# The first load of a scale-and-add kernel: descriptors of 4 KB instead of 8 KB

One Trainium2 chip, one core. The metric is the device time of one execution in microseconds, lower is better. All runs quoted are of one state (fast; the granted clock was 1.0 in each).

## The reference

```python
B, S, D = 1024, 16, 512          # x, y: bf16 [1024, 16, 512]; gamma: bf16 [512]
def reference(x, y, gamma):
    return x + gamma * y
```

x and y are 16.8 MB each, and the result is as large: 50.33 MB have to pass between HBM and the core's memory, with very little arithmetic.

## The kernel before

The 16384 rows of 1 KB are cut into three blocks so that each of the 128 partitions has 8, 60 and 60 rows, contiguous in HBM. One transfer moves one block. All loads go through one queue (SyncE's), all stores through another (ScalarE's, together with gamma).

```python
BLOCKS = [8, 60, 60]
# ... (cut)
SP = [                       # loads in this order: tensor, first row, end row, (place in x's buffer)
    ('y', 0, 8),
    ('y', 8, 68),
    ('x', 8, 68, 0),
    ('y', 68, 128),
    ('x', 68, 128, 15),
    ('x', 0, 8, 0),
]
ACT = [('g',), ('s', 8, 68), ('s', 68, 128), ('s', 0, 8)]     # gamma, then the stores
EARLY = (2, 0)               # the first two loads stand at the head of the program
RELEASE = ('x', 68, 128, 15) # stores may start when this load has landed
DVE = [('m', 0), ('m', 1), ('m', 2), ('a', 2), ('a', 1), ('m', 3), ('a', 3), ('a', 0)]
# ... (cut)
            elif kind == "x":
                to = x_sb[:, w[3] : w[3] + w[2] - w[1], :]
                i = eng.dma_start(out=to, in_=rows_of(xf, w[1], w[2])).then_inc(s_load[w], 16)
            elif kind == "y":
                r = slice(w[1], w[2])
                i = eng.dma_start(out=y_sb[:, r, :], in_=rows_of(yf, w[1], w[2])).then_inc(s_load[w], 16)
            else:
                r = slice(w[1], w[2])
                i = eng.dma_start(out=rows_of(of, w[1], w[2]), in_=y_sb[:, r, :]).then_inc(s_out, 16)
```

VectorE multiplies pieces of y by gamma in place ("m") and adds x to them ("a"); gamma is spread over the partitions by one matmul.

## Time and profile before

| | before |
|---|---|
| time, median of 3 runs | 119.86 us (119.83 to 119.91) |
| span of the profiled run | 118.5 us |
| share of the 16 DMA engines' time in packets | 65.8% + 32.7% |
| VectorE busy | 59% |
| first packet starts / first load landed | 1.04 / 4.82 us |
| last packet ends / last store landed | 118.11 / 118.50 us |

The first two rows tell how fast the program is; the third tells why. The other times are in us from the issue of the first load; those with two decimals are from the trace's records of packets and of semaphore increments. A load or store has landed when the last of its 16 increments is recorded. The lines themselves are in the prediction.

### The profile page before, as it was taken

What the parts mean: (1) busy time and instruction counts of PE and PEld (TensorE: products, weight loads), DVE (VectorE), ACT (ScalarE), POOL (GpSimd) and SP (SyncE); (2) the same over time, 40 slices, a digit from 0 to 9 for tenths busy, and PEclk for the clock granted to TensorE, in tenths of its full rate; (3) what the DMA queues carried; (4) which work ended last, traced back from release to release, by engine and by line L of the source; (5) the groups of instructions that cost most, each with busy time, mean ns of one, the idle gap of its engine ahead of it and who ended that gap; (6) DMA issues with size and microseconds to landing.
All of it is one profiled execution on the core that took longest, in us unless ns stands there. A gap on an engine that the chain in (4) does not pass through costs nothing. (4 is left out here: it accounts for less than half of the span.)

```text
span 118.5 us, 81 instructions
## 1 busy us (share of the span) xinstructions
PE 0.6 (0%) x1; PEld 0.1 (0%) x1; DVE 70.1 (59%) x10; POOL 0.2 (0%) x4
## 2 busy tenths in 40 slices
PE   0001000000000000000000000000000000000000
PEld 0000000000000000000000000000000000000000
DVE  0005400299999399999499999469999950000000
POOL 0000000000000000000000000000000000000000
DMA  5999779779779779978977977897797797797787
GB/s 180 506 602 394 332 332 663 332 332 663 332 332 663 332 332 601 394 332 352 643 332 332 663 332 332 384 633 332 332 663 332 332 663 332 332 663 332 332 365 321
DMA packets 1298, 50.33 MB, mean 425 GB/s; under 512 B 145, under 2 KB 146, under 8 KB 146
## 3 DMA queue, kind: packets, MB, share of 16 engines
q1 hardware_dynamic: 864, 33.55, 65.8%
q10 hardware_dynamic: 434, 16.78, 32.7%
HBM read 33.56 MB, written 16.78 MB: 425 GB/s over the span
## 5 line engine op out<-in xcount | busy, mean ns | idle before, releaser
L170 DVE TENSOR_TENSOR y_sb<-y_sb,gamma_sb 128x4096 bf16<-128x4096 bf16 (+3 forms) x4 | 34.7, 8689 | 11.9 <-DVEq L33 11.9
L179 DVE TENSOR_TENSOR y_sb<-x_sb,y_sb 128x23040 bf16<-128x23040 bf16 (+3 forms) x4 | 34.6, 8688 | 4.5 <-DVEq L33 4.5
L146 DVE CAST gamma_sb<-gamma_ps 128x512 bf16<-128x512 f32 x1 | 0.7, 690 | 7.9 <-DVEq L33 7.9
L141 DVE MEMSET ones_row<- 1x128 bf16 x1 | 0.2, 165 | 2.0 <-PEq L49 2.0
L144 PE MATMUL gamma_ps<-gamma_row,ones_row 1*128 1x512 bf16 x1 | 0.6, 581 | 9.3 <-PEq L33 9.3
L144 PEld LDWEIGHTS gamma_ps<-gamma_row,ones_row 1*128 1x128 bf16 x1 | 0.1, 97 | 9.3 <-issue 9.3
L208 POOL MEMSET const-bfloat16-1.0<- 128x1 bf16 x1 | 0.1, 102 | 0.0
L208 POOL MEMSET const-uint8-127<- 128x1 uint8 x1 | 0.1, 102 | 0.0
L208 POOL MEMSET const-float32-0.0<- 128x1 f32 x1 | 0.1, 99 | 0.2 <-issue 0.2
L208 POOL MEMSET const-float32-1.0<- 128x1 f32 x1 | 0.1, 99 | 0.0
## 6 DMA issues: line engine op xcount, KB each, us to landing
y_sb<-in_y_dram SPq DMA_DIRECT2D x2, 7680.0 KB, 39.8
x_sb<-in_x_dram SPq DMA_DIRECT2D x2, 7680.0 KB, 31.5
out_dram<-y_sb ACTq DMA_DIRECT2D x2, 7680.0 KB, 21.0
y_sb<-in_y_dram SPq DMA_DIRECT2D x1, 1024.0 KB, 4.8
x_sb<-in_x_dram SPq DMA_DIRECT2D x1, 1024.0 KB, 22.3
out_dram<-y_sb ACTq DMA_DIRECT2D x1, 1024.0 KB, 22.1
gamma_row<-in_gamma_dram ACTq DMA_DIRECT2D x1, 1.0 KB
```

The lines of the kernel that those rows point to most:

```text
L141: nc.vector.memset(ones_row, 1.0).then_inc(s_ones, 1)
L144: nc.tensor.matmul(gamma_ps, ones_row, gamma_row, start=True, stop=True).then_inc(s_ps, 1)
L146: nc.vector.tensor_copy(out=gamma_sb, in_=gamma_ps).then_inc(s_dve, 1)
L170: nc.vector.tensor_tensor(out=yt, in0=yt, in1=g, op=MULT).then_inc(s_dve, 1)
L179: nc.vector.tensor_tensor(out=yt, in0=xt, in1=yt, op=ADD).then_inc(s_add, 1)
L208: nc = _bacc.Bacc("TRN2", target_bir_lowering=False, num_devices=1)
```

## The change

The intent is to let the first load run in smaller pieces: 8 contiguous rows of a partition, 8 KB, become two descriptors of 4 KB. (A descriptor is one contiguous piece of a transfer; the trace records each as one packet.) Bytes, order, waits and all other transfers stay as they are.

```diff
+FIRST_BYTES = 4096
@@
             elif kind == "y":
                 r = slice(w[1], w[2])
-                i = eng.dma_start(out=y_sb[:, r, :], in_=rows_of(yf, w[1], w[2])).then_inc(s_load[w], 16)
+                cap = FIRST_BYTES if w == y_loads[0] else None
+                i = eng.dma_start(out=y_sb[:, r, :], in_=rows_of(yf, w[1], w[2]), max_dma_last_dim=cap).then_inc(s_load[w], 16)
```

## The prediction

> **What bounds the kernel now.** I read the page's header and busy lines first, then the slices, then the table of DMA queues, then the waits, then the timeline of VectorE, and at last the DMA view in short windows.
>
> ```profile
> DVE  0005400299999399999499999469999950000000
> DMA  5999779779779779978977977897797797797787
> DMA packets 1298, 50.33 MB, mean 425 GB/s; under 512 B 145, under 2 KB 146, under 8 KB 146
> q1 hardware_dynamic: 864, 33.55, 65.8%
> q10 hardware_dynamic: 434, 16.78, 32.7%
> y_sb<-in_y_dram SPq DMA_DIRECT2D x1, 1024.0 KB, 4.8
> ```
>
> VectorE has empty slices at both ends and gaps between. The two DMA queues together take 65.8% + 32.7% = 98.5% of the time of all 16 DMA engines. The 7s in the slice line are an artefact: a packet is booked where it starts, and most packets here last almost a slice (shown below). 1298 packets are what the kernel's shapes give if one contiguous row of a partition is one packet: nine transfers x 128 = 1152, one for gamma, and 145 of 4 bytes which tell of the end (9 x 16 + 1). So the first load is 128 packets of 8192 bytes, 8 on each engine. In the trace's packet records I chained each packet to the one that ended within 12 ns of its start: this gives 16 chains, 3.146 MB each, with no gap above 20 ns from an engine's first packet (1.035 to 1.832 us) to its last (ends 117.84 to 118.11 us). The kernel is 16 DMA engines that work without a pause, and whichever ends last sets the time.
>
> The waits and the timeline tell how much room VectorE has:
>
> ```profile
> DVE y_sb L170 <- DVEq L33: 11.9, 3, 9.8
> 11.02 2.29 DVE L170 TENSOR_TENSOR y_sb<-y_sb,gamma_sb 128x4096 bf16<-128x4096 bf16 x1 [0.26 <-DVEq L33]
> 23.10 16.23 DVE L170 TENSOR_TENSOR y_sb<-y_sb,gamma_sb 128x7680 bf16<-128x7680 bf16 x2 [9.79 <-DVEq L33]
> 41.36 16.23 DVE L179 TENSOR_TENSOR y_sb<-x_sb,y_sb 128x23040 bf16<-128x23040 bf16 x2 [2.04 <-DVEq L33]
> 59.40 16.16 DVE L170 TENSOR_TENSOR y_sb<-y_sb,gamma_sb 128x30720 bf16<-128x30720 bf16 x1 [1.81 <-DVEq L33]
> ```
>
> The first load lands at 4.8 us, its multiply starts only at 11.02 us because gamma comes late (its semaphore fills at 9.2 us), and after it VectorE is idle 9.8 us until the second y load lands (22.96 us by the trace). Every later stretch starts with an idle gap that a landing ends. So neither the first load nor its multiply is urgent; what counts of the first load is how long it holds the DMA engines.
>
> **What the Trainium skill says.** (1) "DMA: Bandwidth & Descriptors", Where 436 GB/s comes from: 435 GB/s is the ceiling of 16 ports. The trace agrees: 425 GB/s over the whole span. (2) Same page, Why small descriptors are slow (HBM only): a fixed overhead of about 3 cycles for each packet,[...] which matters for packets of a few hundred bytes.[...] (3) Same page, The descriptor swizzle: engines 0 to 7 serve partitions 0 to 63, engines 8 to 15 the others, four partitions in a row each, and hardware generation splits the same way. The trace fits: the 16 chains start in two groups of eight, 1.035 to 1.450 us and 1.667 to 1.832 us, as if descriptors were made in the order of partitions. (4) Same page, Queues, rings and completion order: engines alternate between queues at packet boundaries only. That fits gamma's wait: issued at 1.9 us on the other queue, its 1 KB packet starts at 6.56 us, after a packet of 61440 bytes, and its semaphore packet starts at 8.87 us, one such packet later.
>
> **The change part by part.** Instruction for instruction both programs are the same on every engine; only the first load's pattern turns from 128x4096 into 128x2x2048 elements.
>
> *Removed and added packets.* 128 packets of 8192 bytes go, 256 of 4096 bytes come: 16 on each engine instead of 8. The cost of one comes from two windows of the before trace, the first with packets of 8192 bytes alone (2.5 to 4 us), the second with 61440 bytes alone (60 to 76 us):
>
> ```profile
> DMA packets 77, 0.63 MB, mean 421 GB/s; under 512 B 0, under 2 KB 0, under 8 KB 0
> q1 hardware_dynamic: 77, 0.63, 99.6%
> ...
> DMA packets 112, 6.88 MB, mean 430 GB/s; under 512 B 0, under 2 KB 0, under 8 KB 0
> q1 hardware_dynamic: 112, 6.88, 99.2%
> ```
>
> 16 engines x 1.5 us x 99.6% / 77 = 310 ns for 8192 bytes; 16 x 16 us x 99.2% / 112 = 2267 ns for 61440 bytes. The packet records say 309 and 2267, with each start 3 ns before the previous end, so 306 and 2264 from start to start. The difference, 1958 ns for 53248 bytes, is 27.2 bytes per ns; 8192 bytes at that rate are 301 ns, so about 5 ns are fixed. A packet of 4096 bytes should then take 150.6 + 5 = 155.6 ns start to start, and 16 of them 2490 ns against 8 x 306 = 2448 ns: **+0.04 us** on every engine. As no engine ever pauses, this is fully on the path: +0.04 us of 119.86, or 0.03%.
>
> *Moved: the landing of the first load.* 4.8 us becomes about 4.86 us. VectorE wants it at 11 us, so this costs nothing.
>
> *Moved: gamma.* Its place in the alternation may change, since packet boundaries on the first load come every 156 ns instead of 306. If gamma's packet gets in before the first packet of 61440 bytes, gamma lands up to 4.7 us earlier (about 4.5 us instead of 9.2), and the first multiply starts near 6.3 us. It would then only idle longer until 22.96 us: no gain.
>
> *Moved: the ramp.* This is the one part whose size I cannot work out. At present the first packets take 361 to 1108 ns instead of 309, yet all end between 2.05 and 2.28 us; taking off 309 ns, data flow begins on all engines between 1.74 and 1.97 us, wherever they started. If the cause is a common delay before the first data, smaller descriptors change nothing. I take this as the most likely, and the sum is **+0.04 us, 119.90 us**. I put the point a little higher, at 119.95, because the first rival below is larger than the second.
>
> **The rivals.**
> *The generator is slow for each descriptor.* The eight later engines start 0.632 us after the eight earlier ones (1.667 against 1.035), the last 0.797 us after the first. If this is the pace at which descriptors are made, about 64 of them between engine 0 and engine 8 (9.9 ns each), then twice as many make engine 8 start at 1.035 + 1.264 = 2.30 us, and engine 15 at 1.035 + 1.594 = 2.63 us. With the 52 to 146 ns which these later engines need before data flows, their flow begins at about 2.35 to 2.75 us instead of 1.74 to 1.97: +0.6 to +0.8 us, never made up because each engine has its fixed share and the last one sets the end. Time: 120.5 to 120.7. For it: the two groups. Against it: the flow begins at one common moment although the early group started 0.6 us before, and from the second packet on no engine is short of descriptors. About 35%.
> *The first data flows earlier.* If a first packet must be read whole before the write starts, half the size saves up to half of 301 ns: -0.15 + 0.04, 119.75 us. Against it: the shortest first packet took 361 ns, only 52 over a later one, so there is little left to save. About 20%.
> *VectorE or the release of the stores becomes the bound.* The stores' release follows the landing of the last large x load (77.4 us), which moves with the stream itself. VectorE has 1.8 us or more of idle time ahead of each later stretch. I see no way in which this could cost anything: under 3%, some tenths of a us.
>
> **Range and chances.** Neutral gives 119.85 to 120.0 (45%), the slow generator 120.5 to 120.7 (35%), the early flow about 119.7 to 119.8 (20%); runs of the kernel before lie within 0.08 us. I predict 119.95 us, 8 in 10 within 119.65 and 120.65. Two per cent is 2.4 us, or the whole time for which the first load holds the engines; no rival comes near. Faster 1%, same 98%, slower 1%.
>
> **What would show it right or wrong.** The header should count 1426 packets, 402 of them under 8 KB, and queue q1 992. A window within the first load should give about 156 to 159 ns a packet and a rate near 420 GB/s; a much lower rate there means a fixed cost above my 5 ns. The landing of the first load tells the ramp: about 4.86 us if neutral, 4.7 if the flow starts earlier, 5.4 to 5.6 if generation is slow, and then with eight engines that start after 2.2 us. The second y load's landing (22.96 us) and the last store should move by the same amount. The first multiply may start at 6 us or at 11 us without any effect on the end. I am wrong if the chains of packets get pauses after the first load, if packets of 61440 bytes change from 2267 ns, or if the end moves by more than the first load's landing does.

## The result, and the profile after

The changed kernel took 120.07 us (median of 6 runs, 120.02 to 120.15) against 119.88 us (6 runs, 119.76 to 120.05): ratio 1.0014, 95% interval 1.0001 to 1.0027. A ratio here is the mean time of one kernel's fast runs over that of the other's of the same rounds, so it is not quite the ratio of the quoted medians. Twice more on other occasions (below) the ratio was 1.0009 and 1.0008. So the change costs 0.1 to 0.2 us: the same within 2%, and if anything slower.

The header, the load queue and the landing of the first load on the page of the kernel after (the queue's columns are packets, MB, share of the 16 engines' time; the last line's are KB and us from issue to landing):

```profile
DMA packets 1426, 50.33 MB, mean 424 GB/s; under 512 B 145, under 2 KB 146, under 8 KB 402
q1 hardware_dynamic: 992, 33.55, 65.9%
y_sb<-in_y_dram SPq DMA_DIRECT2D x1, 1024.0 KB, 5.0
```

The counts are the ones foreseen, 128 packets more, and the load's landing is at 5.0 us instead of 4.8. Its packets, in a window of the DMA view of the kernel after from 2.3 to 3.6 us, where all of them are of this load:

```profile
DMA packets 130, 0.53 MB, mean 410 GB/s; under 512 B 0, under 2 KB 0, under 8 KB 130
q1 hardware_dynamic: 130, 0.53, 99.7%
```

16 engines x 1.3 us x 99.7% / 130 = 160 ns for 4096 bytes, where nearly all records say 159: the working's 155.6 from start to start, and the 3 ns by which packets overlap in the records. VectorE's timeline of the kernel after, to be set beside the one of before (start, duration, instruction, and in brackets the idle time ahead of it):

```profile
11.20 2.29 DVE L173 TENSOR_TENSOR y_sb<-y_sb,gamma_sb 128x4096 bf16<-128x4096 bf16 x1 [0.26 <-DVEq L35]
23.27 16.23 DVE L173 TENSOR_TENSOR y_sb<-y_sb,gamma_sb 128x7680 bf16<-128x7680 bf16 x2 [9.77 <-DVEq L35]
41.53 16.23 DVE L182 TENSOR_TENSOR y_sb<-x_sb,y_sb 128x23040 bf16<-128x23040 bf16 x2 [2.04 <-DVEq L35]
59.56 16.16 DVE L173 TENSOR_TENSOR y_sb<-y_sb,gamma_sb 128x30720 bf16<-128x30720 bf16 x1 [1.80 <-DVEq L35]
```

Every start is 0.16 to 0.18 us later than before, and the idle times ahead are the same to 0.02 us. The shift is there when the first load lands (4.99 against 4.82 us), and at the second load's landing (23.13 against 22.96) it is the same (0.17 us). Nothing is lost or won back by VectorE.

What was not foreseen is in a view that I had not opened before predicting: the first issue by itself, before and then after (durations in ns: min/median/max of this one instruction).

```profile
L130 SPq DMA_DIRECT2D y_sb<-in_y_dram x1: 372/372/372, 0.0 to 0.0; - x1
```

```profile
L133 SPq DMA_DIRECT2D y_sb<-in_y_dram x1: 425/425/425, 0.0 to 0.0; - x1
```

The instruction that issues the first load now takes 425 ns instead of 372, and the first packet starts at 1.095 instead of 1.035 us.

### The profile page after: what moved, and what is told of

The parts are those of the page before. It is cut to its first block, busy times and chain, and to the rows that moved or that the text cites. A ratio compares the mean times of both kernels' runs of the same rounds, so it can differ in the third digit from the quotient of the medians.

```text
span 118.7 us, 81 instructions
## 1 busy us (share of the span) xinstructions
PE 0.6 (0%) x1; PEld 0.1 (0%) x1; DVE 70.1 (59%) x10; POOL 0.2 (0%) x4
```

## The experiments

**Theory after the result.** Three parts: a longer issue at the very head of the program (+0.05 us), the packets (+0.04 us), and a more uneven start of the 16 engines. **Rivals:** chance; packets of 4 KB that cost more than 5 ns each and explain it alone; a descriptor generator that is slow for each descriptor.

For all but the repeats, the size was made a table, used for loads (and in one run for the stores):

```diff
-FIRST_BYTES = 4096
+CAPS = {...}                 # (tensor, first row, end row): bytes
-    ... max_dma_last_dim=cap)
+    ... max_dma_last_dim=CAPS.get(w[:3]))
```

Results, each against the kernel before on the same chip (medians; n runs):

| run | CAPS or edit | us | ratio (95%) |
|---|---|---|---|
| before_again | none | 119.94 (5) | 1.0002 (0.9988 to 1.0015) |
| after_again | the change | 120.05 (5) | 1.0009 (0.9997 to 1.0022) |
| after_third | the change | 120.02 (6) | 1.0008 (0.9991 to 1.0025) |
| first_2k | y 0..8: 2048 | 120.21 (6) | 1.0023 (1.0005 to 1.0041) |
| first_1k | y 0..8: 1024 | 120.50 (5) | 1.0047 (1.0034 to 1.0059) |
| last_4k | x 0..8: 4096 | 119.95 (6) | 1.0000 (0.9982 to 1.0018) |
| last_1k | x 0..8: 1024 | 120.41 (5) | 1.0040 (1.0027 to 1.0052) |
| big_first_8k | order of first two loads | 120.19 (5) | 1.0018 (1.0004 to 1.0031) |
| big_first_4k | the same, y 0..8: 4096 | 120.32 (4) | 1.0028 (1.0015 to 1.0042) |
| big_first_1k | the same, y 0..8: 1024 | 120.59 (4) | 1.0056 (1.0042 to 1.0070) |
| loads_4k | all loads but the first: 4096 | 124.28 (6) | 1.0362 (1.0349 to 1.0375) |
| stores_4k | both large stores: 4096 | 121.96 (4) | 1.0171 (1.0151 to 1.0191) |

Before was 119.91, 119.90 and 119.89 us (medians).

**The repeats.** No edit; the kernels before and after once and twice more.

> The kernel before, unchanged, to learn how well it repeats and how its ramp varies. Every theory: ratio to before 1.000 within 0.0015. In the profile I expect data to flow on the 16 engines from 1.74 to 1.97 us again (spread near 0.24 us) and the first load's landing at 4.80 to 4.85 us. If the spread comes out as anything between 0.2 and 0.5 us, the uneven start after the change is chance and not its doing.

> The changed kernel, unchanged. Main theory: the loss of about 0.19 us has three parts, packets +0.04, a longer issue of the first load (425 instead of 372 ns, +0.05), and a more uneven start of the engines (data flow from 1.64 to 2.08 us instead of 1.74 to 1.97, +0.05 to +0.1 on the latest). It should repeat: +0.1 to +0.25 us, first packet near 1.09 us, four engines that start after 2.0 us. Rival (noise): the time is within 0.05 us of before and the profile's ramp looks like that of before.

> The changed kernel a third time, for its scatter: time +0.1 to +0.2 us; first issue 415 to 425 ns, first packet 1.07 to 1.10 us, landing of the first load 4.95 to 5.05 us. If the latest engine's data flow begins below 2.06 us here, the more uneven start seen in the first two profiles is chance, and the loss is issue and packets alone.

The loss repeats in sign and is 0.13 to 0.19 us by the medians, though two of the three intervals reach 1. The profiles separate it better. There are six starts with a first load of 8 KB packets (before, before_again, and four runs below whose change comes later) and three of the changed kernel; in us:

| | first load in 8 KB (6 profiles) | in 4 KB (3 profiles) | difference of means |
|---|---|---|---|
| first issue takes | 0.361 to 0.382 | 0.412 to 0.425 | +0.044 |
| first packet starts | 1.002 to 1.035 | 1.061 to 1.095 | +0.055 |
| data flow begins on the latest engine | 1.97 to 2.15 | 2.08 to 2.18 | +0.09 |
| last packet of the first load ends | 4.428 to 4.600 | 4.566 to 4.619 | +0.09 |
| first load landed, latest engine | 4.76 to 4.96 | 4.956 to 4.992 | +0.13 |

The times are from the trace's records; data flow on an engine begins at the end of its first packet less the time that one of its later packets takes. The times of the issue and of the first packet do not overlap between the two groups. The start of the latest engine does; most of its +0.09 is the 0.055 of the later first packet, and the rest is within what two executions of one kernel differ by. So the uneven start that I read out of the first pair of profiles is not established: the spread alone (0.24 us before) was 0.77 us in before_again, where flow began on different engines between 1.29 and 2.06 us; I had expected 0.24 again. By the mark that I had set for after_third (below 2.06 us would have shown it to be chance) it was not refuted either: 2.18 us. But in after_third some engines moved a first packet by 1.35 us and paused afterwards; counted back from the last packet's end (4.576 us, 16 packets of 155.6 ns), the latest start is 2.09 us. Counted back in the same way in all nine, the latest start moves by +0.05 us in the means, as the first packet does.

**More descriptors in the same place.** 2 KB and 1 KB.

> First load in descriptors of 2 KB, 32 packets an engine. Main theory: issue near 420 ns as with 4 KB and 1 KB, so it belongs to the added dimension and not to the number of descriptors, +0.06 us; packets 32 x (75.3 + 4.9) = 2.57 us, +0.12 us; landing of the first load at 5.0 to 5.1 us; time +0.15 to +0.3 us. Rival (issue or start grows with the number of descriptors): first packet after 1.15 us, first load landing after 5.2 us.

> First load in descriptors of 1 KB, 64 packets an engine instead of 8. Main theory: 64 x (37.7 + 4.9) ns = 2.72 us against 2.45, +0.28 us; issue +0.05; uneven start +0.1 to +0.3 if it grows with the number of descriptors: together +0.4 to +0.65 us, about 120.3 to 120.5. Rival (a packet costs more than 5 ns, all of the loss of the change is packets: 0.19 us / 8 = 24 ns each): 56 x 24 = +1.3 us. Rival (generation at 9.9 ns for each descriptor, the slow generator of the prediction): 1024 x 9.9 = 10 us for the first load, +7 us or more.

The first packets start at 1.097 and 1.090 us, with issues of 425 and 417 ns: the same as with 4 KB. So the longer first issue goes with the added dimension of the pattern, not with the number of descriptors. What does grow with their number is the issue of the second load, right behind it: 424 ns in before, 459 or 460 in the three runs with 4 KB, 497 with 2 KB, 568 with 1 KB; its packets are not wanted before 4 us. With 2 KB the first load lands at 5.06 us, as the main theory expected. Nor is generation the bound: 1024 descriptors are handled with the first load landing at 5.3 us, by the issue table of first_1k:

```profile
y_sb<-in_y_dram SPq DMA_DIRECT2D x1, 1024.0 KB, 5.3
```

At the 9.9 ns each that I had taken from the staggered starts, they would have needed 10 us. The slow generator is ruled out. The times, +0.3 and +0.6 us, are at the upper end of what the main theory expected. In first_1k the records show one reason: packets of 1 KB take 46 ns until 4.0 us, then 49 to 52 in the mean, with VectorE idle and no packet of another queue under way.

**The same bytes where the issue is off the path.** The last load, x 0..8, is issued at 57.6 us and its packets run from 76.5 us.

> The change's own descriptor size on the other small load: the last one, whose issue is long past when its turn comes, in 4 KB; the first stays at 8 KB. Main theory (of the change's loss some 0.06 us is the longer issue of a first instruction with one more dimension, 0.04 us packets, the rest start scatter): first issue 372 ns and first packet at 1.00 to 1.04 us as before, +0.04 us in the end, too little to tell from before by time. Rival (the loss belongs to packets of 4 KB wherever they are): +0.15 us or more. It also adds another start with 8 KB packets.

> First load at 8 KB as before; instead the last load (the same 8 rows of x), whose issue and descriptors are ready long before its turn, in descriptors of 1 KB. Main theory: packets alone, +0.28 us, nothing for issue or start; the difference from first_1k is then what the place at the start of the program costs. Rival (a packet costs 24 ns): +1.3 us. Rival (only the start costs anything): 0. The landing of the last load should move by the same amount, that of all earlier loads not at all.

The added dimension lengthens this issue as well (383 ns in last_1k and last_4k, 328 in before), but 20 us ahead of need. It does so for both large stores too (407 and 379 ns in stores_4k, 369 and 339 in before), but not for a load issued right behind another: 423 to 434 ns in second place, with the dimension (big_first_4k, big_first_1k, loads_4k) and without. last_4k: 119.95 us, +0.06 by the medians, ratio 1.0000; of its 256 packets the mean was 159.8 ns. By time it cannot be told from before, while the change in the first place reads +0.13 to +0.19; but its interval, 0.2 us either way, doesn't exclude that. last_1k cost 0.5 us instead of the 0.28 expected. Its packets say why: up to 78 us they followed each other every 42.3 ns as worked out, then slowed. The DMA view in two windows of last_1k, 76.9 to 77.8 us and 78.6 to 79.4 us:

```profile
DMA packets 335, 0.33 MB, mean 372 GB/s; under 512 B 8, under 2 KB 335, under 8 KB 335
q1 hardware_dynamic: 335, 0.33, 105.0%
...
DMA packets 275, 0.28 MB, mean 352 GB/s; under 512 B 0, under 2 KB 275, under 8 KB 275
q1 hardware_dynamic: 275, 0.28, 110.5%
```

16 x 0.9 us x 105.0% / 335 = 45 ns recorded in the first (46 in the records, with 8 short semaphore packets in the mean), 16 x 0.8 x 110.5% / 275 = 51 ns in the second.

**The small load second in the queue.** The edit:

```diff
 SP = [
-    ('y', 0, 8),
     ('y', 8, 68),
+    ('y', 0, 8),
-DVE = [('m', 0), ('m', 1), ('m', 2), ...
+DVE = [('m', 1), ('m', 2), ('m', 0), ...
```

> The order of the first two loads turned round: the 60 rows of y first (one packet of 61440 bytes per partition), the 8 rows second, still 8 KB each; their multiplies follow in the same order. The small load is then neither in the ramp nor is its issue on the path. Main theory (the small load at the head of the queue only costs what its packets, issue and start cost): bytes and packet counts are those of before, so within 0.1 us of before. Rival (a small first load is what makes the engines start sooner): +0.2 us or more. It is the base for the next two runs.

> As big_first_8k, with the 8 rows of y, now second in the queue, in descriptors of 4 KB. Main theory: 8 more packets an engine at 4.9 ns, +0.04 us against big_first_8k, as issue and start are no longer on the path; the landing of this load and the next moves by 0.03 to 0.06 us. Rival (packets of 4 KB cost the whole 0.17 us that the change cost wherever they stand): +0.17 us in the landings against big_first_8k.

> As big_first_8k, with these 8 rows in descriptors of 1 KB, at a time when no other queue has work. In last_1k the packets took 42.3 ns from start to start until 78.1 us and up to 57 later, once the store's queue was filled. Main theory (the extra there comes of a second queue or of VectorE's reads beside it): here all take about 42.3 ns, the load holds an engine 64 x 42.3 = 2.71 us, +0.26 us against big_first_8k. Rival (packets of 1 KB vary anyway): +0.45 us as in last_1k.

big_first_8k was 0.3 us slower than before. Its profile shows one engine on which data flow began only at 2.61 us, the next at 2.10; but this is the slowest of its five runs (120.46; the others 120.04 to 120.21), so a single profile doesn't settle a cause. I had expected no difference; a small load at the head seems to be worth about 0.2 us here (ratio 1.0018), and why is not settled. big_first_4k: the runs scatter too much (119.99 to 120.41 us) to show 0.04 us, and its profile fell on the fastest. The packets are clean: all 128 of 8 KB took exactly 309 ns in the one, all 256 of 4 KB took exactly 159 in the other. From start to start these are 305.9 and 155.3 ns in the mean, so 8 x 305.9 = 2447 against 16 x 155.3 = 2485 ns an engine: +0.04 us. big_first_1k went against the main theory: packets of 1 KB took 46 ns until 21.7 us and 51 to 53 in the mean after, although no other queue had work. So the second queue is not what slows them. (VectorE began to multiply at 20.96 us in this run, so it does not rule out the other half of that theory; first_1k above does.)

**The packet cost, multiplied.**

> First load at 8 KB, all five later loads in descriptors of 4 KB (15 for each partition of the large ones): 4 x 112 + 8 = 456 more packets on each engine, so the cost of one is measured 57 times as large as in the change. Main theory (4.9 ns each, fully on the path): +2.2 us, 122.1 us, ratio 1.019. Rival (24 ns each): +10.9 us. Rival (packet cost hidden by the engines' pipelining once they run): 0.

> All loads as before, the two large stores in descriptors of 4 KB: 224 more packets on each engine. loads_4k cost 4.4 us for 456 (9.6 ns each): there packets of 4 KB took 159 ns up to 8.8 us and 164 in the mean after. Theory A (the extra 5 ns are of reading HBM in small pieces): stores keep 159 ns, +1.1 us, 121.0 us. Theory B (the extra 5 ns are of generating or fetching descriptors in long streams, for either direction): about 164 ns, +2.15 us, 122.05 us.

loads_4k cost 4.4 us, twice what I expected, and not five times as the rival has it. Two windows of its DMA view, 5 to 8 us and 20 to 40 us:

```profile
DMA packets 313, 1.27 MB, mean 425 GB/s; under 512 B 1, under 2 KB 2, under 8 KB 313
q1 hardware_dynamic: 311, 1.27, 103.0%
...
DMA packets 2015, 8.19 MB, mean 409 GB/s; under 512 B 16, under 2 KB 16, under 8 KB 2015
q1 hardware_dynamic: 2015, 8.19, 102.5%
```

16 x 3 us x 103.0% / 311 = 159 ns in the first; 16 x 20 x 102.5% / 2015 = 163 in the second (16 semaphore packets of 9 ns pull the mean down; the records give 164.0). In the records every packet takes 159 from 5 to 8.5 us; from about 9 us to the end of the loads they take 159 to 172. Per added packet: 4.38 us / 456 = 9.6 ns. In stores_4k it is 2.07 us / 224 = 9.2 ns, so it is not reading that does it (theory A falls). Its DMA view from 80 to 92 us (first store) and from 100 to 115 us (second):

```profile
DMA packets 1235, 5.06 MB, mean 422 GB/s; under 512 B 0, under 2 KB 0, under 8 KB 1235
q10 hardware_dynamic: 1235, 5.06, 102.3%
...
DMA packets 1498, 6.14 MB, mean 409 GB/s; under 512 B 0, under 2 KB 0, under 8 KB 1498
q10 hardware_dynamic: 1498, 6.14, 102.0%
```

16 x 12 x 102.3% / 1235 = 159.0 ns and 16 x 15 x 102.0% / 1498 = 163.4. The 9.2 ns are thus a mean over unequal stretches: 159.0 ns up to 92 us, 163.3 from 98 us on, and between 94 and 98 us some packets of up to 298 ns. What sets in there stays open. It isn't VectorE's work beside it: in loads_4k VectorE was idle from 10.2 to 24.3 us, by its timeline:

```profile
7.90 2.29 DVE L172 TENSOR_TENSOR y_sb<-y_sb,gamma_sb 128x4096 bf16<-128x4096 bf16 x1 [0.26 <-DVEq L35]
24.30 4.16 DVE L172 TENSOR_TENSOR y_sb<-y_sb,gamma_sb 128x7680 bf16<-128x7680 bf16 x1 [14.10 <-DVEq L35]
```

The same lines show gamma getting in earlier (first multiply at 7.9 instead of 11.0 us) and VectorE waiting the longer for the next load: an early gamma is worth nothing, as the prediction said.

SyncE's own timeline in loads_4k:

```profile
1.92 8.43 SPq L129 DMA_DIRECT2D x_sb<-in_x_dram  x1
10.40 18.99 SPq L132 DMA_DIRECT2D y_sb<-in_y_dram  x1
```

The issues of the third and fourth load take 8.43 and 18.99 us; in before they take 0.33 and 0.43 (in big_first_1k the third takes 13.68). So many descriptors do hold the issuing engine. It cost nothing here, as no DMA engine had a gap between packets after its start; what SyncE is held by is not shown.

No run beat the kernel before.

## Why the prediction was right or wrong

Right in outcome: 120.07 us lies within 119.65 to 120.65, and "same" was given 98%. Luck has a part in it: the range reached up to 120.65 for the sake of the slow generator, which was wrong, and 120.07 lies in none of the three branches (neutral 119.85 to 120.0, slow generator 120.5 to 120.7, early flow 119.7 to 119.8). The sum itself, +0.04 us, is under a third of the 0.13 to 0.19 measured.

- *The DMA engines are the bound, without slack.* Right: the shift of the first load's landing (0.17 us in the first pair) is found at each later landing of a load (0.15 to 0.17), and at the end it is 0.21 (118.50 to 118.71 us). The prediction had named an end that moves by more than that landing as a sign of being wrong; over the profiles it does not: from the first load's landing to the last store's it is 113.69 and 113.74 us in the two of before, 113.70 to 113.73 in the three of the changed kernel.
- *Packets, +0.04 us.* Right: 159 ns recorded, 3 ns of them overlap, as worked out; in big_first_4k +0.04 us an engine. The fixed 5 ns hold only for the first stretch of a stream; in long streams it was 9 to 10 ns. The first load's 16 packets an engine stay at 159 ns from 2.3 us on in after_again and after_third; in the first profile of the changed kernel 13 of them took 161 to 281.
- *Landing and gamma cost nothing.* Right: gamma didn't get in earlier (the first multiply moved with the rest, 11.02 to 11.20 us), and where it did, in loads_4k, it bought nothing. Even with a packet boundary about every 0.16 us, gamma's packet starts there only at 5.51 us, when the first load's packets are over (4.57 to 4.62 us in the changed kernel). If gamma is ready no earlier in before, smaller packets of the first load could not let it in, and of the wait until 6.56 us that the prediction puts down to the alternation of queues only the last 1.05 us can belong to it; what holds gamma until then is not shown. The prediction also took the page's packets, which hold several descriptors, for the trace's, which are one each, so its fit with that page is looser than it says.
- *The ramp changes nothing in the likely case, so +0.04 in all.* Here the sum was too small. It counted packets and flow and had no term for the issue: "Instruction for instruction both programs are the same on every engine" was true of the list, but not of the durations. The pattern's second dimension makes the issue 0.044 us longer, and as this issue stands ahead of everything, the first packet is 0.055 us later. With packets this makes about 0.10 us, and the end of the first load's last packet moved by 0.09 (means of 3 and 6 profiles). Its landing moved by 0.13; the rest lies between that packet's end and the landing (0.33 to 0.40 us with 8 KB, 0.37 to 0.43 with 4 KB) and is left open. That the later first packet is what moves the stream is argued from these means: the single profiles scatter by as much (4.43 to 4.60 us with 8 KB), and no run changed the issue alone.
- *The slow generator.* Wrong, and I gave it 35%: eight times the descriptors landed 0.5 us later than 8 KB (first_1k), not 7 us. The two groups of starting engines are no sign of the pace of generation; their times varied from run to run with the kernel unchanged.
- *Earlier flow.* Not seen: the first load landed at 4.956 us or later in all three profiles of the changed kernel, at 4.955 or earlier in all six with 8 KB, so the two groups all but touch.

## What to carry to other kernels

Where DMA engines work without a pause, each added packet is fully on the path: ask for as few and as large descriptors as the layout gives, and find the cost of one from two packet sizes in the trace before changing anything. Here a first issue longer by 0.044 us came with a first packet later by 0.055 us, so look at the duration of a program's first issue and not only at what it moves; the same longer issue could be afforded by a transfer issued 20 us ahead of need. For differences of 0.1 us compare several profiles of each kernel: landings in one pair of profiles mix the effect with the scatter of the start.

## What the Trainium skill lacked or had wrong

- "DMA: Bandwidth & Descriptors", Why small descriptors are slow (HBM only), puts the packet overhead at about 3 cycles and advises packing only up to 256 B. Here it was about 5 ns in fresh streams (3 cycles at the 850 MHz that the page gives for the fabric would be 3.5 ns, an estimate; the page does not say that its cycles are of that clock), but 9.6 ns a packet over long loads in 4 KB and 9.2 ns over long stores: in loads_4k 3.6% of the time for packets 16 times as large as that limit. The page doesn't tell of the rise (159 ns a packet of 4 KB at first, 164 later), and no run here settled its cause.
- The same page doesn't give how long the issue of one transfer takes by its pattern: 361 to 382 ns for the first load as one run per partition, 412 to 425 ns with one more dimension, whether 2, 4 or 8 descriptors per partition. The pattern is not all: other loads of one run per partition took 327 to 339 ns (x) and 423 to 434 (the second load, y), and with many descriptors of 4 KB on the way 8.43 and 18.99 us.
- The same page, The descriptor swizzle, fits the even split over 16 engines (3.146 MB each; which partitions an engine serves no trace here shows), but the order in which engines start is not fixed by it: with one kernel, eight engines started by 1.45 us in one run and six by 1.30, the seventh at 1.64, in another.
